# Adding a token's own value on TensorE instead of VectorE in eleven units of an RWKV-then-MoE kernel

## The chip, the cores and the metric

The kernel runs on one core of one Trainium2 chip. The metric is the device time of one execution in microseconds, lower is better; where nothing else is said, a time is in microseconds and counts from the start of the profiled span. The engines are named as in the profile: PE is TensorE, DVE is VectorE, ACT is ScalarE, POOL is GpSimd, SP is SyncE, which issues most of the transfers. PEld is the weight load of PE.

## What is computed

A recurrent attention (RWKV) is followed by a mixture of experts with one expert for each token. The first part, cut to what matters:

```python
for t in range(S):                      # B=4 sequences, H=8 heads, S=768, D=48
    kt, vt, rt = k[:, :, t], v[:, :, t], r[:, :, t]
    cur = einsum('bhd,bhe->bhde', u * kt, vt)
    y[:, :, t] = einsum('bhd,bhde->bhe', rt, state + cur)
    state = w[:, :, None] * state + einsum('bhd,bhe->bhde', kt, vt)
```

The term with `cur` is the token's own: for each head it is the scalar d = sum(r * u * k) times the token's own v. The second part takes x, the heads of y side by side (3072 tokens of 384), and computes `logits = x @ w_gate + modality_bias`, the expert with the greatest logit and its softmax weight, and for each token `weight * (relu(x @ w1[e]) @ w2[e])` of that expert (8 experts, 384 to 1024 to 384).

## The kernel before

The first part works on units: a unit is 128 tokens of one of the 4 sequences, all 8 heads, and there are 24, in the order of the chunks, so that units 0 to 3 are the first chunk. The recurrence is written as products within a chunk, and a state that is handed from chunk to chunk. For each unit PE makes the scores (line 383, into two banks `psc`), DVE masks them (line 389, `at`), and PE sums into one bank, `py`, the state's part (line 413, not in the first chunk) and the chunk's part (line 420). It then makes the new state's part in bank `pst` (line 431; for units 8 to 13 line 426 first adds the faded old state by a product) and, in the same bank, the scalars d of the next unit (line 352, "bonus"). DVE copies d out (line 357), and ACT scales the token's own v by it, head by head, into `dv` (line 369, eight pieces in two halves; from unit 9 to 13 POOL does the second half, line 365).

`token`, the function that changes, makes x: it adds `dv` to `py` (line 439, DVE, 128x384 in f32), and ACT sums the squares of x (line 454). From that sum DVE derives a power of two (lines 287 and 289, `ebx` and `sx`), ACT writes the high half of x as f16 (line 484), DVE the low half (line 488), and SP turns both by a DMA transpose (line 493) for the routing.

A loop of steps runs over the units. In step i the engines get, in this order: the scores of unit i+1; `token` of unit i-1; the copy of d of unit i; the state of unit i-1 out of `pst` (line 469 on ACT in the first chunk, line 467 on DVE later, line 474 on ACT for units 8 to 13); the keys of unit i+2 (line 343); the power of two for unit i-1; the first half of `dv` of unit i; the high half of unit i-1; the masks of unit i+1; the second half of `dv`; the low half of unit i-1 and its transpose; and `values` of unit i, which is lines 413 to 431 and the bonus of unit i+1. Pieces of routing work are put in between at marked places. Each engine runs its own list strictly in this order; the order is written by hand and no scheduler changes it. `py` has two buffers, so the sums of unit i wait until the low half of unit i-2 has been read; `pst` has one.

From step 8 on the mixture of experts starts beside this: the routing tables (lines 637 to 657 on DVE, at the end of step 8), the loads of the first expert's weights (line 852, from SP), their squares (line 855, ACT), their scale (lines 869 and 872) and their split into two f16 halves (lines 885 and 890). Step 13 also runs the first half of an expert's products for the first 128 tokens (line 944) between the scores and `values`.

Ahead of the scores of units 1 to 13 PE runs products that write nothing anybody reads (line 377): 128x128 ones in f16 times 128x512 ones, into the banks that the scores then overwrite. There are 6 for units 1 to 8 and 2 for units 9 to 13.

Of the kernel before, what the change touches and what calls it, by code (L numbers as in the profile page):

```python
# [41 lines left out]
DENSE = 6  # L42
FADED = range(8, 14)
SHARED = range(9, 14)

NE = 9
EARLY = 3
# [12 lines left out]
class _Kernel:  # L60
# [298 lines left out]
    def own(self, i, q):  # L359
        nc, u = self.nc, self.ctx_[i]  # L360
        if q == 0:
            u["dv"] = self.a.tile([P, DM], F32, tag="dv", name=f"dv{i}")
        if q and i in SHARED:
            half = lambda t: t[:, DM // 2 :].rearrange("p (h e) -> p h e", e=D)
# [6 lines left out]
    def scores(self, i):  # L371
        nc, u = self.nc, self.ctx_[i]
        u["ps"] = [self.ps_a.tile([P, 512], F32, tag="big", name=f"psc{i}_{j}") for j in range(2)]
        if 0 < i < BARE:

            for q in range(2 if i - 1 in FADED else DENSE):
                nc.tensor.matmul(u["ps"][q % 2], self.ones16, self.warm, start=True, stop=True)

        for pr in range(NPR):
            for q in range(2):  # L380
                s = slice(64 * q, 64 * q + 64)
                for j, r in enumerate(HALVES):
                    nc.tensor.matmul(u["ps"][j][s, pr * P : (pr + 1) * P], u["kc"][r, pr, s], u["rc"][r, pr, :], start=True, stop=True)  # L383
# [51 lines left out]
    def token(self, i):  # L435
        nc, a, u = self.nc, self.a, self.ctx_[i]
        b, c = self.units[i]
        u["x"] = u["py"][:, :DM]
        nc.vector.tensor_add(u["x"], u["x"], u["dv"])
        n = [hi - lo for lo, hi in GROUPS if lo == i]  # L440
        if n:

            new = lambda n, sh, dt=F32, **k: a.tile(sh, dt, tag=n, name=f"{n}{i}", **k)
            self.grp = dict(
                n=n[0],
                lo=i,
                row=new("row", [P, B, RW], I16, bufs=3),
                xT=new("xT", [P, B, 2 * DC, P], F16),
                ssq=new("ssq", [P, B]),
                sx=new("sx", [P, B]),  # L450
            )
        u["g"], u["at_g"] = self.grp, i - self.grp["lo"]
        u["x16"] = self.grp["row"][:, u["at_g"], : 2 * DM].bitcast(F16)
        nc.scalar.activation(u["x16"][:, :DM], u["x"], AF.Square, accum_out=self.grp["ssq"][:, u["at_g"] : u["at_g"] + 1])
# [981 lines left out]
```

## Time and profile before

| | us |
|---|---|
| median of 3 runs | 363.95 (361.91 to 366.08) |
| the profiled execution | 359.0 |
| its span, first to last instruction | 357.2 |
| PE busy in the span | 334.1 (94%) |
| DVE busy | 227.1 (64%) |
| ACT busy | 172.4 (48%) |
| line 439, 24 of them on DVE, median of one | 0.554 |
| line 377, 58 records on PE, first and last start | 10.3 and 79.1 |

Busy is the share of time in which an engine runs at least one instruction; the units and the routing lie in the first 180 us or so, the experts behind them. A row of the order of time has the start, the length, the engine, the line, what it writes and reads, its shape, how many instructions were merged into the row, and in brackets the idle time of the engine ahead of it with what ended that. A length of several merged rows is from the first one's start to the last one's end.

### The profile page before, as it was taken

How to read it: one execution, taken by the hardware profiler on the slowest of the kernel's cores; microseconds unless marked ns; L12 is line 12 of the kernel's file. 1: busy time of each engine (PE TensorE's matmuls, PEld its weight loads, DVE VectorE, ACT ScalarE, POOL GpSimd, SP SyncE). 2: the span in 40 equal slices, each digit the busy share in tenths (PEclk: the TensorE clock that was granted, in tenths of full speed). 3: DMA queues.
4: the chain of work that ended last, by engine and by line, in shares of the span. 5: the costliest groups of instructions: out<-in, count | busy, mean ns of one | idle time of the engine just before them, and what ended most of it. 6: DMA issues, size and time to landing. Idle time of an engine off the chain costs nothing. (4 is left out here: it accounts for less than half of the span.)

```text
span 357.2 us, 15050 instructions
## 1 busy us (share of the span) xinstructions
PE 334.1 (94%) x5415; PEld 267.0 (75%) x5415; DVE 227.1 (64%) x751; ACT 172.4 (48%) x457; POOL 168.8 (47%) x233
## 2 busy tenths in 40 slices
PE   7989998996999999999999999998999999999792
PEld 3667787776978796988977677776778888777671
DVE  6998999879498958596558733249423233334950
ACT  7469664657466576566432222255222222257620
POOL 8897578747556773444175611136111121111821
PEclk9999999698799999999999999999999999999999
DMA  6999879999947999753345621125721112112120
GB/s 188 279 226 175 180 214 168 330 280 204 237 115 179 231 239 284 173 120 99 92 110 156 247 68 45 44 53 170 245 65 45 44 44 66 44 26 63 22 57 5
DMA packets 60749, 50.29 MB, mean 141 GB/s; under 512 B 46872, under 2 KB 54311, under 8 KB 60448
## 3 DMA queue, kind: packets, MB, share of 16 engines
q1 hardware_dynamic: 57504, 40.21, 50.5%
q0 software_dynamic: 3200, 9.47, 7.3%
q8 instruction: 30, 0.49, 0.6%
q14 instruction: 15, 0.12, 0.1%
HBM read 28.39 MB, written 11.83 MB: 113 GB/s over the span
## 5 line engine op out<-in xcount | busy, mean ns | idle before, releaser
L944 PEld LDWEIGHTS <-whi 128*128 128x128 f16 x1248 | 73.5, 99 | 3.8 <-issue 1.0
L1018 PEld LDWEIGHTS <-hh 128*128 128x128 f16 x416 | 38.9, 98 | 29.9 <-issue 4.4
L944 PE MATMUL phb<-mxT,whi 128*128 128x128 f16 x768 | 50.7, 219 | 0.0
L369 ACT ACTIVATE dv<-kv,d 128x48 f32<-128x48 f32 x172 | 43.0, 324 | 4.2 <-DVE d L357 2.3
L944 PEld LDWEIGHTS <-wlo 128*128 128x128 f16 x624 | 38.4, 99 | 1.5 <-DVE wlo L890 1.5
L336 POOL TENSOR_TENSOR rk<-rc,kc 128x512 f32<-128x512 f32 x20 | 25.9, 1296 | 27.2 <-DVE ebx L287 13.7
L953 DVE SCALAR_TENSOR_TENSOR hl<-phb,hh 128x256 f16<-128x256 f32 (+1 forms) x48 | 24.2, 512 | 22.7 <-ACT hh L948 18.4
L948 ACT ACTIVATE hh<-phb 128x256 f16<-128x256 f32 (+1 forms) x48 | 21.5, 453 | 34.3 <-PE L944 15.0
L324 POOL TENSOR_TENSOR rc<-ud,powr 128x512 f32<-128x512 f32 (+1 forms) x27 | 31.7, 1182 | 9.2 <-DMA ud<-in_pd 7.5
L1028 DVE TENSOR_SCALAR fac<-mt,wf 128x1 f32<-128x1 f32 x17 | 3.6, 212 | 49.1 <-ACT otb L904 45.6
L389 DVE TENSOR_TENSOR at<-psc,mask 128x512 f32<-128x512 f32 x48 | 31.6, 679 | 1.9 <-PE psc L383 1.8
L904 ACT ACTIVATE otb<-po,fac 128x384 f32<-128x384 f32 x16 | 9.2, 577 | 46.0 <-PE phb L944 42.0
L608 POOL DMA_INDIRECT rows<-row,posi x24 | 26.2, 1093 | 11.0 <-issue 3.4
L1023 PEld LDWEIGHTS <-hl 128*128 128x128 f16 x208 | 19.2, 98 | 16.3 <-issue 3.9
L944 PE MATMUL phb<-mxT,wlo 128*128 128x128 f16 x384 | 29.6, 219 | 1.2 <-DVE wlo L890 1.2
L1018 PE MATMUL po<-wlo,hh 128*128 128x384 f16 x136 | 28.0, 326 | 2.7 <-DVE wlo L890 2.6
L913 POOL TENSOR_TENSOR seenb<-otb,putb 128x1 int32<-128x1 int32 x16 | 5.0, 310 | 53.0 <-ACT otb L904 50.2
L383 PE MATMUL psc<-rc,kc 64*64 64x128 f32 (+1 forms) x768 | 28.7, 288 | 0.4 <-DVE kc L343 0.3
L420 PE MATMUL py<-kv,at 128*64 128x48 f32 x768 | 27.1, 224 | 1.5 <-issue 1.5
L383 PEld LDWEIGHTS psc<-rc,kc 64*64 64x64 f32 (+1 forms) x768 | 22.1, 140 | 8.5 <-issue 3.1
L944 PE MATMUL phs<-mxT,whi 128*128 128x128 f16 x432 | 28.4, 224 | 0.0
L890 DVE SCALAR_TENSOR_TENSOR wlo<-raw,ws,whi 128x1024 f16<-128x1024 f32 (+1 forms) x18 | 27.8, 1590 | 0.8 <-ACT whi L885 0.8
(261 smaller groups left out, 672.9 us busy)
## 6 DMA issues: line engine op xcount, KB each, us to landing
ud<-in_pd SPq DMA_DIRECT2D x24, 384.0 KB, 4.3
kv<-in_pt SPq DMA_DIRECT2D x24, 384.0 KB, 5.3
raw<-in_w SPq DMA_DIRECT2D x12, 512.0 KB, 6.4
raw<-in_w SPq DMA_DIRECT2D x2, 1536.0 KB, 6.5
rows<-pad SPq DMA_DIRECT2D x10, 193.0 KB, 2.4
rows<-row,posi POOLq DMA_INDIRECT x24, 5.1
xT<-row SPq DMA_TRANSPOSE x23, 2.8
xn<-rows SPq DMA_TRANSPOSE x17
```

The source lines that it names most:

```text
L324: nc.gpsimd.tensor_mul(u["rc"][:, s], u["rT"][:, s], self.powr[:, s])
L336: (eng or nc.gpsimd).tensor_mul(u["rk"], u["rc"], u["kc"])
L369: nc.scalar.activation(u["dv"][:, sl], u["v"][:, sl], AF.Copy, scale=u["d"][:, h : h + 1])
L383: nc.tensor.matmul(u["ps"][j][s, pr * P : (pr + 1) * P], u["kc"][r, pr, s], u["rc"][r, pr, :], start=True, stop=True)
L389: nc.vector.tensor_mul(u["at"][:, j * NPR : (j + 1) * NPR, :], u["ps"][j].rearrange("p (q t) -> p q t", q=NPR), self.mask.unsqueeze(1).to_ ...
L420: nc.tensor.matmul(py[t, sl], u["at"][:, j * NPR + pr, t], u["v"][:, sl], start=c == h == 0, stop=h == H - 1, skip_group_check=True)
L608: i = nc.gpsimd.indirect_dma_start(out=self.rows, out_offset=bass.IndirectOffsetOnAxis(ap=u["posi"][:, b : b + 1], axis=0), in_=u["row"][: ...
L890: self.nc.vector.scalar_tensor_tensor(self.wlo[:, sl], self.raw[:, sl], sc, self.whi[:, sl], ALU.mult, ALU.subtract)
L944: self.nc.tensor.matmul(ph[:, q * P : (q + 1) * P], w[:, c0 : c0 + P], self.xT[:, xq, t * P : (t + 1) * P], start=i == q == 0, stop=i == l ...
L948: self.nc.scalar.activation(self.hh[:, f0 : f0 + fb, t * P : (t + 1) * P], p3, AF.Relu)
L953: self.nc.vector.scalar_tensor_tensor(self.hl[:, f0 : f0 + fb, r], p3, 0.0, self.hh[:, f0 : f0 + fb, r], ALU.max, ALU.subtract)
L1018: self.nc.tensor.matmul(po[:, :DM], self.hh[:, f, t * P : (t + 1) * P], w[:, c0 : c0 + DM], start=n == q == f == 0, stop=False)
```

## The change

```diff
+ADDED = range(2, 13)
...
-            for q in range(2 if i - 1 in FADED else DENSE):
+            for q in range(1 if i - 1 in FADED else DENSE // 2 if i - 2 in ADDED else DENSE):
                 nc.tensor.matmul(u["ps"][q % 2], self.ones16, self.warm, start=True, stop=True)
...
         u["x"] = u["py"][:, :DM]
-        nc.vector.tensor_add(u["x"], u["x"], u["dv"])
+        if i in ADDED:
+            nc.tensor.matmul(u["x"], self.id32, u["dv"], start=False, stop=True, skip_group_check=True)
+        else:
+            nc.vector.tensor_add(u["x"], u["x"], u["dv"])
```

`DENSE` is 6 and `FADED` is units 8 to 13. In units 2 to 12 the addition on DVE goes, and PE multiplies `dv` by the f32 identity and accumulates onto the bank of `py`. The product stands where `token` is called, so on PE behind the scores of unit i+1 (and, in step 13, behind line 944's products) and ahead of `values`. The products that write nothing become 3 for units 4 to 8 and 1 for units 9 to 13; units 1 to 3 keep their 6. The lines of the changed kernel stand one to four further down.

On PE, in step 4, around the end of the scores of unit 5 (`psc5`) and the start of the sums of unit 4 (`py4`), before:

```order
L383 MATMUL psc5_1_681<-rc5_501,kc5_608 64x128
L413 MATMUL py4_754<-st1_96,rc4_401 64x96 x8
L420 MATMUL py4_754<-kv4_278,at4_627 64x48 x16
L431 MATMUL pst4_779<-kv4_278,kt0_91 64x48
L431 MATMUL pst4_779<-kv4_278,kt0_91 48x48
```

and now, with the product of unit 3:

```order
L384 MATMUL psc5_1_678<-rc5_501,kc5_605 64x128
L441 MATMUL py3_641<-dv3_618,id32_138 128x384
L414 MATMUL py4_748<-st1_96,rc4_401 64x96 x8
L421 MATMUL py4_748<-kv4_278,at4_624 64x48 x16
L432 MATMUL pst4_773<-kv4_278,kt0_91 64x48
L432 MATMUL pst4_773<-kv4_278,kt0_91 48x48
```

The product of the unit before has come in between; it reads `dv3`, which ACT writes in step 3.

On DVE, at the end of step 7 and the start of step 8 (`ebx6` and `sx4` are the power of two, `row4` the low half, `pr0` the routing's sums, `d8` the scalars of unit 8), before:

```order
L287 TENSOR_SCALAR ebx6_1112<-ssq4_827 128x1
L289 TENSOR_SCALAR sx4_828<-ebx6_1112 128x1
L389 TENSOR_TENSOR at8_1126<-psc8_0_1066,mask_143 128x512
L389 TENSOR_TENSOR at8_1126<-psc8_1_1067,mask_143 128x512
L488 SCALAR_TENSOR_TENSOR row4_825<-py6_1016,sx4_828,row4_825 128x384
L439 TENSOR_TENSOR py7_1135<-py7_1135,dv7_1120 128x384
L574 TENSOR_TENSOR pr0_910<-pr0_910,base_160 128x32
L357 COPY d8_1213<-pst7_1160 128x8
```

and now:

```order
L288 TENSOR_SCALAR ebx6_1097<-ssq4_818 128x1
L290 TENSOR_SCALAR sx4_819<-ebx6_1097 128x1
L390 TENSOR_TENSOR at8_1111<-psc8_0_1054,mask_143 128x512
L390 TENSOR_TENSOR at8_1111<-psc8_1_1055,mask_143 128x512
L492 SCALAR_TENSOR_TENSOR row4_816<-py6_1004,sx4_819,row4_816 128x384
L578 TENSOR_TENSOR pr0_901<-pr0_901,base_160 128x32
L358 COPY d8_1197<-pst7_1145 128x8
```

The addition is gone and nothing else has moved: the power of two (line 288 now) still stands ahead of the masks and waits for the sum of squares, which now waits for PE's product.

On PE in step 13, before:

```order
L944 MATMUL phs0_0_1923<-mxT_262,wlo_267 128x128
L869 LDWEIGHTS onesb_145
L869 MATMUL pww2_1973<-wssq_268,onesb_145 128x3
L413 MATMUL py13_2011<-st1_96,rc13_1523 64x96 x8
L420 MATMUL py13_2011<-kv13_1392,at13_1815 64x48 x16
```

and now:

```order
L948 MATMUL phs0_0_1903<-mxT_262,wlo_267 128x128
L441 MATMUL py12_1808<-dv12_1788,id32_138 128x384
L873 LDWEIGHTS onesb_145
L873 MATMUL pww2_1953<-wssq_268,onesb_145 128x3
L414 MATMUL py13_1991<-st1_96,rc13_1505 64x96 x8
L421 MATMUL py13_1991<-kv13_1375,at13_1795 64x48 x16
```

The product of unit 12 stands behind the expert's products and ahead of the sum for the weights' scale.

## The prediction

> **What bounds the kernel now.** I read the page first (its shares are means over stages with different limits), then a table of busy time by step of the loop, and then the order of time around the steps that the change touches. The question is whether TensorE (PE), VectorE (DVE) or ScalarE (ACT) sets the pace in those steps. Step i is one pass of the loop over units. It starts on PE with the empty products ahead of the scores of unit i+1; I cut the trace there, from step 3 (25.66) to step 13 (87.76, which I let run into step 14's scores). The columns are PE, weight loads, DVE, ACT, POOL, then the granted clock.
>
> ```profile
> 25.66:30.05 4.39, 4.39 (x104) 3.31 (x102) 3.20 (x9) 3.85 (x14) 3.67 (x5) 1.00 1.00 198
> 30.05:35.11 5.06, 5.06 (x120) 3.97 (x119) 4.48 (x10) 4.98 (x21) 3.24 (x3) 1.00 0.81 153
> 35.11:41.03 5.92, 5.75 (x145) 4.59 (x143) 5.81 (x14) 3.90 (x15) 2.52 (x4) 1.00 0.67 170
> 41.03:46.07 5.04, 5.04 (x124) 3.95 (x121) 4.95 (x18) 3.92 (x15) 4.77 (x8) 1.00 1.11 242
> 46.07:51.41 5.34, 5.34 (x131) 4.25 (x130) 5.18 (x16) 3.61 (x14) 3.14 (x5) 1.00 0.71 173
> 51.41:56.68 5.27, 5.27 (x129) 4.51 (x126) 5.14 (x19) 3.37 (x13) 4.10 (x5) 1.00 1.13 193
> 56.68:64.74 8.06, 6.31 (x148) 5.39 (x147) 7.78 (x34) 2.43 (x8) 7.39 (x8) 0.90 1.15 233
> ...
> 87.76:100.15 12.39, 12.39 (x219) 11.78 (x218) 6.79 (x16) 6.44 (x14) 8.58 (x9) 0.75 1.11 237
> ```
>
> In steps 3 to 8 PE has no idle time but for 0.17 us in step 5: five of the six rows show busy equal to the length. DVE is nearly as full from step 5 on (5.14 of 5.27 in step 8), but PE never waits for it except in that 0.17. So a VectorE addition taken away there buys nothing by itself, and what PE gains or loses in work goes straight into the time. From step 9 on PE waits, for these things:
>
> ```profile
> 56.40 0.16 DVE L637 SCALAR_TENSOR_TENSOR pr<-pr,idxf 128x8 f32<-128x8 f32 x1
> ...
> 59.66 0.57 DVE L439 TENSOR_TENSOR py<-py,dv 128x384 f32<-128x384 f32 x1
> ...
> 60.26 0.49 ACT L454 ACTIVATE row<-py 128x384 f16<-128x384 f32 x1 [4.00 <-DVE py L439]
> ...
> 60.70 0.15 DVE L357 COPY d<-pst 128x8 f32<-128x8 f32 x1
> ...
> 60.88 0.48 ACT L474 COPY st<-pst 112x384 f32<-112x384 f32 x1
> ...
> 61.41 1.02 PE L426 MATMUL pst<-st,wd 112*112 112x96 f32 x8 [1.36 <-ACT st L474]
> ...
> 78.67 0.16 PE L352 MATMUL pst<-uw,rk 112*64 112x2 f32 x1 [0.80 <-issue]
> ...
> 87.35 0.48 PE L352 MATMUL pst<-uw,rk 112*64 112x2 f32 x6 [3.07 <-issue]
> ```
>
> In step 9 the addition stands on DVE behind the routing work that begins at 56.40; the square waits 4.00 for it, the copy L474 stands behind the square on ACT, and PE's L426 waits 1.36 for that copy. The stalls of 0.80 and 3.07 end by nothing that PE, DVE or ACT does (the releaser is "issue"). Step 13 is gap-free on PE again.
>
> **The change part by part.** Prices first, from these rows of steps 4 and 8.
>
> ```profile
> 30.05 1.47 PE L377 MATMUL psc<-warm 128*128 128x512 f16 x6
> ...
> 31.45 1.10 PE L383 MATMUL psc<-rc,kc 64*64 64x128 f32 x32
> ...
> 51.41 0.59 PE L377 MATMUL psc<-warm 128*128 128x512 f16 x2
> ...
> 51.94 1.10 PE L383 MATMUL psc<-rc,kc 64*64 64x128 f32 x32
> ...
> 52.97 0.88 PE L413 MATMUL py<-st,rc 112*64 112x96 f32 x16
> ...
> 53.68 1.09 PE L420 MATMUL py<-kv,at 128*64 128x48 f32 x32
> ```
>
> An empty product: six hold the scores back by 31.45 - 30.05 = 1.40, two by 0.53, so one costs 0.87/4 = 0.22. Steps 3 to 7 lose three each (-0.66), steps 8 to 12 one each (-0.22).
>
> The f32 product with the identity, which the trace has not: the code issues 8 products at L413 and the row counts 16 records, so an f32 product is streamed twice, and 384 columns become 768. Lower bound: 768 columns at the f16 pace of 0.22 per 512, 0.33. Upper bound: the 8 records of L426 at 61.41 cover the whole array and also make 8 x 96 = 768 columns, in 1.02, with four times as many weight loads. Between them, L413's 16 records use half of the array each; two side by side are again 768 columns, and from its start to the next shape's is 53.68 - 52.97 = 0.71, changes of shape included. I take 0.71, which is also the nearest in kind, and keep 0.33 and 1.02 for the range.
>
> Steps 3 to 8, on PE: six products, +4.26; empty products, 5 x 0.66 + 0.22 = -3.52. Net +0.74.
>
> The addition (0.57 on DVE, 11 times) is hidden now by PE's own work in steps 3 to 8, so taking it away is worth nothing there. But the square now comes after the scores and the product, and everything queued behind it on ACT with it. Step 3:
>
> ```profile
> 26.14 0.49 ACT L454 ACTIVATE row<-py 128x384 f16<-128x384 f32 x1 [1.38 <-DVE py L439]
> ...
> 27.06 1.10 PE L383 MATMUL psc<-rc,kc 64*64 64x128 f32 x32
> ...
> 27.50 0.31 ACT L469 COPY st<-pst 48x192 f32<-48x192 f32 x1
> ...
> 28.09 1.14 PE L420 MATMUL py<-kv,at 128*64 128x48 f32 x32
> ...
> 29.06 0.57 PE L431 MATMUL pst<-kv,kt 128*64 128x48 f32 x15
> ```
>
> The product starts at 28.09 - 0.66 = 27.43, its result is there some 0.88 later (L413's whole length), so the square starts at 28.31 and not at 26.14: 2.17 later. The copy L469 that frees the state's bank is queued behind it and ends at 27.81 + 2.17 = 29.98, where L431 would be ready at 29.06 - 0.66 + 0.71 = 29.11. A new wait of 0.87, which does not exist now; the products of the bonus and the whole next step are queued behind it on PE, and DVE waits for the bonus. The rest of ACT's queue (the token's value for the next product, and the cast that VectorE's low part waits for) is then 2.17 late while PE is only 0.92 late. Step 4 has no room to catch up: ACT is 4.98 of 5.06 busy there. The difference of 1.25 comes back as PE waiting for the token's value at step 4's product or for the low part ahead of step 5's L413, which is where the 0.17 of step 5 lies. Behind the waiting product or L413 stands the rest of the unit on PE, and behind that DVE's next copy of d. I take all 1.25; the ends are 0, if steps 4 and 5 absorb it, and 2.2. In steps 6 to 8 nothing more: ACT is busy 3.4 to 3.9 of over 5 and follows. Sum up to the end of step 8: 0.74 + 0.87 + 1.25 = +2.86.
>
> Step 9: product and empty product, +0.49. The square no longer waits for DVE, so the copy L474 is out of the way early; the other thing that L426 needs is the copy of d at 60.70, which moves with DVE's queue, at most 2.86 later and 0.57 sooner for the addition, to 63.0. PE is there 2.86 + 0.49 after its old arrival at 61.41 - 1.36 = 60.05, at 63.4, so the 1.36 is gone. Net -0.87, sum +1.99.
>
> Steps 10 to 12: +0.49 each, 1.47, priced at nothing, because the stalls of 0.80 and 3.07 stand behind them and end at a time that PE does not set. If that cover goes, +1.47.
>
> Step 13 has no empty products and PE is gap-free through it. Its product stands ahead of the sum of squares that the weights' scale needs, for which DVE waits:
>
> ```profile
> 93.77 0.16 DVE L872 TENSOR_REDUCE wtotw<-pww 128x1 f32<-128x3 f32 x1 [4.87 <-PE pww L869]
> ```
>
> So +0.71, and up to twice that if it runs at half clock. Sum: 1.99 + 0.71 = **+2.7 us**. No queue of SyncE or GpSimd is given or relieved of anything.
>
> **The clock.** It is at half speed twice in these steps. The rows are stretches as long as the clock's own steps, and what follows two of them.
>
> ```profile
> 59.75:63.17 3.42, 2.06 (x49) 1.84 (x45) 3.42 (x14) 2.43 (x8) 3.12 (x3) 1.00 1.21 103
> 63.17:66.58 3.41, 3.02 (x51) 2.08 (x53) 3.16 (x12) 0.46 (x1) 3.11 (x3) 0.50 1.04 393
> 66.58:70.00 3.42, 3.42 (x62) 3.09 (x54) 2.23 (x10) 3.42 (x11) 3.33 (x4) 0.50 1.04 340
> 76.82:80.24 3.42, 2.62 (x70) 2.02 (x73) 3.42 (x9) 1.58 (x3) 0.02 (x1) 1.00 1.03 278
> 83.65:87.06 3.41, 0.63 (x21) 0.54 (x18) 3.24 (x15) 3.36 (x6) 3.26 (x4) 1.00 1.32 215
> 87.06:90.47 3.41, 3.12 (x46) 2.78 (x46) 1.84 (x4) 1.60 (x7) 3.22 (x3) 0.50 1.00 248
> 90.47:93.89 3.42, 3.42 (x36) 3.33 (x35) 0.12 (x1) 0.25 (x2) 1.64 (x3) 0.50 1.27 165
> ```
>
> PE busy 2.06 of 3.42 cost it the clock, 2.62 of 3.42 (with the stall of 0.80 in it) did not. So a stall between about 0.8 and 1.36 decides, and the stall of step 9 is one that this change should remove. The dense products that go are replaced by a longer dense product, so steps 3 to 8 stay busy.
>
> The Trainium skill ("TensorE: Matmul & The Clock Gate", Part 1) says that the clock falls to half only after at least one idle window of about 3.4 us. This trace does not agree: it fell after a window with 2.06 us of work in it, and the measurement decides. By the page's rule no stall here is long enough to cost the clock, before or after, and the sum would stay +2.7 with no rival from the clock; by the rows there is the first rival below.
>
> **The rivals.** Five rows of ACT come first: the state's copies of step 5, the value and the cast of step 8, and two of step 10, where ACT waits for weights.
>
> ```profile
> 35.68 0.79 ACT L401 ACTIVATE st<-st,w 112x192 f32<-112x192 f32 x2
> ...
> 53.08 1.00 ACT L369 ACTIVATE dv<-kv,d 128x48 f32<-128x48 f32 x4
> ...
> 54.78 0.58 ACT L484 ACTIVATE row<-py,sx 128x384 f16<-128x384 f32 x1 [0.70 <-DVE base L584]
> ...
> 66.12 1.06 ACT L855 ACTIVATE junk<-raw 128x1024 f16<-128x1024 f32 x1 [3.39 <-DMA raw<-in_w]
> ...
> 67.64 0.47 ACT L474 COPY st<-pst 112x384 f32<-112x384 f32 x1
> ```
>
> *Faster: both clock cuts stay away.* With the stall of 1.36 gone, the first cut is; 3.02 + 3.42 of work at half clock would take 3.2 less. And if the stall of 3.07 keeps its end while PE arrives 2 later, it shrinks to about 1, and the second cut goes too: 3.12 + 3.42, 3.3 less. Together 2.7 - 6.5 = -3.8. It decides at a stall of about 1 us in both places. Against it: in step 10 ACT waits 3.39 for weights and holds the copy L474 that L426 needs until 67.64, so that PE could use little of the first 3.2, and the second stall may move along with PE.
>
> *Slower by more than 1%: ACT and the product become a loop.* Product, square, four pieces of the token's value, cast, four pieces, next product: 0.88 + 0.48 + 1.0 + 0.58 + 1.0 = 3.9, and two copies of the state, 0.8, in steps 3 to 7, so 4.7 of PE's 5.1. The loop decides when ACT has 0.4 of other work in a step. At 0.5 more in each of steps 5 to 8, and with the cover of steps 10 to 12 gone, it is 2.7 + 2.0 + 1.47 = +6.2. For it speaks step 4, where ACT is full now; against it, that ACT is at most 3.92 of over 5 busy in steps 5 to 8.
>
> *Hidden: the stalls of steps 11 and 12 swallow all that comes before them.* Then only step 13 counts, +0.7.
>
> **How the numbers follow.** The profiled execution took 359.0 (span 357.2, and 1.8 around it), below all three runs (361.91 to 366.08, median 363.95). The forecast against it is 361.7; against the median, 363.95 + 2.7 = 366.65, which I give as 366.6. The rivals: faster 360.1, slower 370.1, hidden 364.7. Chances: forecast 0.40, slower 0.25, hidden 0.17, faster 0.18. One per cent, 3.6 us, is about what a measurement of this kernel can tell from no change. With the bounds of the unknown costs the forecast runs from 364.0 (seven products that nothing covers, each 0.38 cheaper) to 369.8 (each 0.31 dearer, and 2.2 in place of 1.25), and passes 367.6 in a quarter of its cases. So slower by over 1%: 0.25 + 0.10 = 0.35; faster by over 1%: 0.18; within: 0.47. The range, 360.5 to 370.5, leaves out the farther half of the two outer cases; the likeliest one's own is 364.0 to 369.8.
>
> **What would show it.** Steps 3 to 8 still gap-free or nearly so on PE and some 2.9 longer in all; the identity's product 0.7 from start to the next shape; a wait of PE for ACT's L469 in step 3; no wait at L426 in step 9; the stalls without a releaser in steps 11 and 12 shorter by what PE comes later. It is wrong if the product costs under 0.5, if the clock is never cut, or if PE waits for ACT in each of steps 4 to 8.

## The result, and the profile after

| | before | after |
|---|---|---|
| median, range, runs | 363.58 (361.91 to 366.08), 6 | 368.05 (365.38 to 371.86), 6 |
| the profiled execution, its span | 359.0, 357.2 | 367.79, 365.9 |
| PE busy in the span | 334.1 | 341.2 |

The changed kernel takes 1.0143 of the time before (95% interval 1.0098 to 1.0188): 5.2 us more by the ratio, 4.5 by the medians. It is slower, as the forecast with the largest chance had it, but by more than its +2.7. Here and below, a ratio compares only runs within 1.5% of the fastest of their kernel, so it can lie below the ratio of the medians, which count every run.

The table of busy time by step, as in the prediction (PE, weight loads, DVE, ACT, POOL, granted clock), here from step 3 (28.89) to the scores of step 14:

```profile
28.89:34.39 5.50, 4.76 (x103) 3.39 (x102) 2.40 (x8) 2.73 (x11) 3.45 (x3) 1.00 0.47 119
34.39:40.10 5.71, 5.32 (x119) 3.97 (x118) 3.33 (x9) 5.51 (x23) 2.18 (x2) 1.00 0.56 135
40.10:46.25 6.15, 5.94 (x143) 4.59 (x142) 6.04 (x14) 5.07 (x19) 3.21 (x4) 1.00 0.57 143
46.25:51.49 5.24, 5.24 (x123) 3.96 (x120) 4.51 (x16) 3.17 (x13) 4.98 (x7) 1.00 1.12 236
...
57.03:62.92 5.89, 5.89 (x130) 4.77 (x126) 4.79 (x17) 3.00 (x12) 3.45 (x4) 1.00 1.04 236
62.92:69.58 6.66, 6.59 (x149) 5.42 (x148) 6.42 (x28) 2.44 (x8) 6.06 (x6) 1.00 1.09 225
...
75.62:83.08 7.46, 6.42 (x140) 5.19 (x136) 5.07 (x16) 5.31 (x14) 4.13 (x5) 1.00 1.06 316
83.08:91.97 8.89, 6.05 (x129) 4.91 (x126) 8.68 (x33) 6.64 (x15) 6.06 (x6) 1.00 1.22 200
91.97:105.03 13.06, 12.02 (x222) 10.89 (x220) 8.35 (x16) 6.54 (x16) 8.17 (x8) 0.87 0.87 215
```

The first two columns of numbers are to be compared. PE was full in steps 3 to 8 but for 0.17; now it is idle for 0.74 in step 3, 0.39 in step 4 and 0.21 in step 5, and full again in steps 6 to 8. Step 9 has lost its idle time (8.06 - 6.31 = 1.75 before, 0.07 now). Step 11 has 1.04 idle, and so has the last row, step 13. What those waits are, in the order of time (its first row belongs to the clock, below):

```profile
19.63 0.73 PE L421 MATMUL py<-kv,at 128*64 128x48 f32 x18 [1.75 <-issue]
...
30.67 0.91 PE L441 MATMUL py<-dv,id 128*128 128x384 f32 x2
31.51 1.14 PE L421 MATMUL py<-kv,at 128*64 128x48 f32 x32
31.62 0.49 ACT L458 ACTIVATE row<-py 128x384 f16<-128x384 f32 x1 [6.60 <-PE py L441]
...
32.98 0.31 ACT L473 COPY st<-pst 48x192 f32<-48x192 f32 x1
...
33.36 0.48 PEld L432 LDWEIGHTS pst<-kv,kt 128*64 128x64 f32 x15 [0.84 <-issue]
33.39 0.58 PE L432 MATMUL pst<-kv,kt 128*64 128x48 f32 x15 [0.74 <-POOL kt L332]
...
36.64 0.91 PE L441 MATMUL py<-dv,id 128*128 128x384 f32 x2 [0.39 <-ACT dv L370]
...
43.01 0.88 PE L414 MATMUL py<-st,rc 112*64 112x96 f32 x16 [0.21 <-DVE row L492]
...
77.92 0.49 ACT L458 ACTIVATE row<-py 128x384 f16<-128x384 f32 x1 [1.38 <-PE py L441]
...
78.40 0.47 ACT L478 COPY st<-pst 112x384 f32<-112x384 f32 x1
...
78.92 0.16 PE L873 MATMUL pww<-wssq,onesb 128*128 128x3 bf16 x1 [1.04 <-ACT st L478]
...
91.64 0.40 PE L353 MATMUL pst<-uw,rk 112*64 112x2 f32 x8 [2.84 <-issue]
...
98.53 0.17 PE L873 MATMUL pww<-wssq,onesb 128*128 128x3 bf16 x1 [1.04 <-ACT st L478]
```

In step 3 the square (L458) starts behind the product and not, as before, ahead of the scores; the copy L473 is queued behind it and ends at 33.29, and PE's next products into that bank (L432) start right behind it: their weight load at 33.36, after 0.84 without one, and the products at 33.39, after 0.74 of idle time. The profile does not name the copy as what ended this wait; the order of the three times and the last run below do. In step 4 the product itself waits 0.39 for the token's value, in step 5 the sums wait 0.21 for the low half. The rows from 77.92 to 78.92 are a place that the prediction did not see: the sum of the weights' squares (L873) goes into the bank of `pst`, which the copy L478 has to empty first. The copy stands behind the square, the square behind the product, and PE waits 1.04. The same row with the same 1.04 stands in step 13, at 98.53. The row at 91.64, ahead of the bonus of step 12, is a stall whose end nothing in the profile explains.

The product holds PE for 31.51 - 30.67 = 0.84 until the next shape.

The clock, in windows of its own length:

```profile
17.20:20.60 3.40, 1.65 (x53) 1.51 (x51) 2.48 (x6) 2.29 (x9) 3.17 (x3) 1.00 1.06 255
20.60:24.00 3.40, 3.40 (x29) 2.07 (x25) 2.69 (x6) 2.67 (x9) 2.28 (x3) 0.50 1.25 189
24.00:27.40 3.40, 3.40 (x50) 2.45 (x50) 0.74 (x2) 1.02 (x5) 3.25 (x3) 0.50 0.71 198
88.86:92.28 3.42, 0.64 (x20) 0.62 (x23) 3.25 (x15) 3.30 (x6) 3.23 (x3) 1.00 1.28 187
92.28:95.70 3.42, 3.42 (x52) 3.09 (x42) 2.48 (x3) 0.00 (x0) 3.22 (x4) 0.50 1.00 300
```

Step 9 keeps the clock now, and the cut of step 13 lasts one window and not two. But two windows are lost from 20.6 on, ahead of the first changed instruction (28.89): the stall "issue" of 1.75 at 19.63 falls into the window before. The kernel before has one of 1.48 at the same product and kept its clock there in its profile. That cut accounts for nearly all of the 3.23 by which step 3 starts later (step 2 alone is 3.1 longer), and no changed instruction stands ahead of it. The profile before was a lucky one in this place: eleven of the twelve kernels below have a cut between 20 and 28 as well.

The experts' part seems untouched. From the last bonus product of step 13 to the end the profiled execution of after takes 265.6. In the eight kernels that I ran on one chip it is 264.8 to 267.1 whatever was done to the units. On another chip it is 261.1 to 261.6, and in the profile of before 261.7. So some 3.3 of the 4.6 us by which that profile lies below the six runs before may stand in the experts' part: 97.3 (where that product stands in it) + 265 = 362.3 is near a usual run.

The pair of profiles does not show the whole difference either. Steps 3 to 13, from step 2's last bonus product to step 13's, take 71.78 before and 73.45 after, only 1.67 more. The profile before has four windows at half clock in these steps and the one after has one (a mean granted clock of 0.90 and 0.98), so the waits above are partly paid for by the clock in this pair. What the waits cost is read from the runs, below.

### The profile page after: what moved, and what is told of

Read it like the earlier page. It is cut to its first block, busy times and chain, and to the rows that moved or that the text cites. A ratio compares the mean times of both kernels' runs of the same rounds, so it can differ in the third digit from the quotient of the medians.

```text
span 365.9 us, 15039 instructions
## 1 busy us (share of the span) xinstructions
PE 341.2 (93%) x5417; PEld 267.4 (73%) x5417; DVE 226.9 (62%) x740; ACT 172.6 (47%) x457; POOL 168.4 (46%) x233
## 5 line engine op out<-in xcount | busy, mean ns | idle before, releaser
L1022 PEld LDWEIGHTS <-hh 128*128 128x128 f16 x416 | 38.0, 98 | 33.0 <-ACT hh L952 7.6
L458 ACT ACTIVATE row<-py 128x384 f16<-128x384 f32 x24 | 11.7, 489 | 39.7 <-PE py L441 22.0
L1022 PE MATMUL po<-whi,hh 128*128 128x384 f16 x136 | 28.4, 327 | 0.5 <-ACT hh L952 0.5
```

The costliest lines, as they stand in the source:

```text
L1022: self.nc.tensor.matmul(po[:, :DM], self.hh[:, f, t * P : (t + 1) * P], w[:, c0 : c0 + DM], start=n == q == f == 0, stop=False)
```

## The experiments

Theories as put before the runs: **A**, PE's work sets the pace; **B**, the late square does, through ACT's queue; **C**, the clock decides. Each kernel was timed six or twelve times, beside the kernel before on the same chip. In every table the columns are the ratio with its interval, PE's work against the kernel before (empty product 0.22; product 0.84 behind the scores, 0.74 ahead of them, 0.64 if another product follows: see below), and the mean number of windows of 3.41 at half clock in a run, over all runs, worked out as (1 - mean granted clock) x time / (0.5 x 3.41), here and for the kernel before in the same set.

**First set: one part of the change at a time.**

The empty products as before the change, the product as in it:

```diff
-            for q in range(1 if i - 1 in FADED else DENSE // 2 if i - 2 in ADDED else DENSE):
+            for q in range(2 if i - 1 in FADED else DENSE):
```

> The changed kernel with its empty products as before (6 and 2), so that the product with the identity is the only difference from the kernel before. Theory A (PE's own work sets the pace in steps 3 to 8, the product costs 0.84 there and an empty product 0.22): 15 empty products more in steps 3 to 7 and one more in step 8, 3.5 us, longer than the changed kernel, less the 1.5 us in which PE waits for ACT in steps 3 to 5 now: 370 us, about 1.018 times the kernel before. Theory B (the square that comes later, and ACT's queue behind it, set the pace; PE only waits): the empty products fall into waits, and it takes what the changed kernel takes, 368 us. Theory C (the clock is cut more often because there are fewer empty products): faster than the changed kernel, 364 to 366 us.

The halved empty products alone, the addition on DVE for all units:

> The addition stays on VectorE for all units; only the empty products are halved (3 and 1), as in the changed kernel. Theory A: PE gains 3.5 us in steps 3 to 8 at most; DVE, busy 5.14 of 5.27 in step 8, lets through a part of it: 361 to 363 us, 0.992 to 0.998 times the kernel before. Theory B: no difference from the kernel before, 363.6 us. Theory C: slower than before, 366 us or more, with a lower mean clock.

The whole change, but the product issued in `scores`, between the empty products and the scores:

```diff
             for q in range(1 if i - 1 in FADED else DENSE // 2 if i - 2 in ADDED else DENSE):
                 nc.tensor.matmul(u["ps"][q % 2], self.ones16, self.warm, start=True, stop=True)
+        if i - 2 in ADDED:
+            o = self.ctx_[i - 2]
+            nc.tensor.matmul(o["py"][:, :DM], self.id32, o["dv"], start=False, stop=True, skip_group_check=True)
...
-        if i in ADDED:
-            nc.tensor.matmul(u["x"], self.id32, u["dv"], start=False, stop=True, skip_group_check=True)
-        else:
+        if i not in ADDED:
             nc.vector.tensor_add(u["x"], u["x"], u["dv"])
```

> The changed kernel, but the product with the identity is issued between the empty products and the scores of the same step and not behind the scores, so that the square can start 1.0 us sooner (in step 13, 4.9 us sooner, ahead of the expert's products as well). PE does the same work. Theory A: only the waits for ACT in steps 3, 4, 5 (1.5 us) and part of those ahead of the weights' sum in steps 11 and 13 (2.7 us) go, and the product's own 0.84 stays: 365 to 366 us, 1.005 times the kernel before. Theory B: all of the loss goes, 363.6 us. If the product now waits for the token's value, which ACT writes last in the step before, it is no better than the changed kernel, 368 us.

The same place, but the product goes into the bank that the scores overwrite, and DVE adds for all units:

```diff
+        if i - 2 in ADDED:
+            nc.tensor.matmul(u["ps"][0][:, :DM], self.id32, self.ctx_[i - 2]["dv"], start=True, stop=True)
...
-        if i in ADDED:
-            nc.tensor.matmul(u["x"], self.id32, u["dv"], start=False, stop=True, skip_group_check=True)
-        else:
-            nc.vector.tensor_add(u["x"], u["x"], u["dv"])
+        nc.vector.tensor_add(u["x"], u["x"], u["dv"])
```

> As the one that issues the product ahead of the scores, but the product writes into the scores' bank, where the scores overwrite it, and VectorE adds as in the kernel before. PE's work is that of the changed kernel, and the square waits for DVE as before. Theory A: PE's extra work in steps 3 to 8 is 6 x 0.84 - 3.5 = 1.5 us and in step 13 0.84 at full clock, so 365 to 366 us, like the one before it, since the addition on DVE is hidden. Theory B: as the kernel before, 363.6 us. If the relief of DVE was worth something, this one is slower than the one before it, by up to the 0.55 us of each addition that is not hidden.

| kernel | median | ratio | PE's work | windows, before |
|---|---|---|---|---|
| product only, empty products kept | 372.47 | 1.0252 (1.0177 to 1.0327) | +9.2 | 3.2, 3.7 |
| fewer empty products only | 362.97 | 1.0025 (0.9986 to 1.0063) | -4.4 | 4.8, 3.7 |
| product ahead of the scores | 363.80 | 1.0036 (0.9996 to 1.0075) | +3.7 | 2.6, 3.7 |
| product unused, DVE adds | 363.18 | 1.0040 (1.0001 to 1.0079) | +3.7 | 3.1, 3.7 |

The place of the product is worth 1.1 per cent (1.0143 to 1.0036). That does not yet decide between A and B, because the interval of 1.0036 holds A's 1.005 as well as no loss at all. What DVE is spared is worth nothing that can be measured: used or unused, 1.0036 and 1.0040. The two differ in one thing more, though. In the profile of the used product, step 4 has a wait for the token's value, which ACT writes late in the step before:

```profile
34.47 0.91 PE L382 MATMUL py<-dv,id 128*128 128x384 f32 x2 [1.31 <-ACT dv L370]
```

Theory C as first put falls: the kernel that it had below the change is the slowest, and halving the empty products alone did not cost 1%. Theory A is half refuted and half not: 4.4 us less work on PE gain nothing that can be measured (at best 0.14%), while 4.4 us more behind the late product cost 1.1%, more than A had for it. Both have to be explained.

**Second set: where the late product costs, and whether PE's work has a price.** Three kernels leave the product where the change put it, for a part of the units only, with the halved empty products in all:

```diff
-ADDED = range(2, 13)
+THIN = range(2, 13)
+ADDED = range(2, 5)
...
-            for q in range(1 if i - 1 in FADED else DENSE // 2 if i - 2 in ADDED else DENSE):
+            for q in range(1 if i - 1 in FADED else DENSE // 2 if i - 2 in THIN else DENSE):
```

> The changed kernel, with the product (in the place that the change gave it, behind the scores) for units 2 to 4 alone; units 5 to 12 have VectorE's addition again, and all empty products stay halved. Compare with the kernel that has the halved empty products alone (1.0025) and the changed kernel (1.0143); what is split is the 1.2% between them, 4.3 us. Theory B, late square: the waits that the profile showed for these units, 0.9 at L432 in step 3, 0.5 at step 4's product and 0.3 at L414 in step 5, give 1.7 us, so some 364.5, ratio 1.007. Theory A, PE's work sets the pace: three products of 0.84, 2.5 us, 365.3, ratio 1.009. Where neither holds and the loss comes from later steps, 363, ratio 1.002.

With `ADDED = range(5, 12)`:

> The same with the product for units 5 to 11 alone. Theory B: no wait is seen in steps 6 to 9, only the one of some 1.1 us for the scale of the weights' sum in step 11, so 364, ratio 1.005. Theory A: seven products of 0.84 are 5.9 us, of which the stalls of steps 11 and 12 may swallow two, so 366.5 to 368.5, ratio 1.012 to 1.017.

With `ADDED = range(12, 13)`:

> The same with the product for unit 12 alone; in its step the product stands behind the scores and behind the products of the first expert. Theory B: the square is some 4.9 us later than with VectorE's addition, and the sum of squares for the weights' scale waits for ScalarE, 1.1 to 1.3 us, so 364.2, ratio 1.006. Theory A: one product of 0.84, of which none is covered, 363.8, ratio 1.005. If the end of the loop over units is not what the experts wait for, 363, ratio 1.0025.

And the product ahead of the scores with a second one behind it:

```diff
             nc.tensor.matmul(o["py"][:, :DM], self.id32, o["dv"], start=False, stop=True, skip_group_check=True)
+            nc.tensor.matmul(u["ps"][0][:, :DM], self.id32, o["dv"], start=True, stop=True)
```

> The kernel with the product between the empty products and the scores (1.0036), and a second product of the same operands right behind it, whose result goes into the bank of the scores and is overwritten by them. It adds 11 products of 0.84 to PE, 9.2 us, and moves the square of no unit. Theory A, PE's work goes into the time: 363.8 + 9.2, less what the stalls of steps 11 and 12 swallow (some 2.5), 370 to 373, ratio 1.022 to 1.029. Theory B, PE's work is covered and only the place of the square counts: under 366, ratio below 1.010. If A, the earlier result for the product whose result is unused (1.0040) is hard to understand; if B, the third of the empty products that costs 1.1% behind the late product is so only by making the square later still.

| kernel | median | ratio | PE's work | windows, before |
|---|---|---|---|---|
| units 2 to 4 | 363.25 | 1.0058 (1.0015 to 1.0101) | -1.9 | 5.0, 3.4 |
| units 5 to 11 | 361.95 | 1.0017 (0.9976 to 1.0058) | +1.5 | 2.1, 3.4 |
| unit 12 | 363.78 | 1.0056 (1.0014 to 1.0097) | -3.6 | 4.6, 3.4 |
| product twice | 372.28 | 1.0189 (1.0080 to 1.0299) | +10.8 | 3.3, 3.4 |

Units 2 to 4 and unit 12 lie where B had them, but their intervals hold all three expectations: undecided. Units 5 to 11 are clear: seven late products cost nothing that can be seen, against A's 1.012 to 1.017, although the profile has the wait at the weights' sum, 1.04 in step 11 and 1.44 in step 13. It has something to set against that: PE's wait of 2.4 at the state in step 9, which the two other kernels of this kind have, is not in it, and it loses the clock least. Above the 1.0025 of the halved empty products the parts make 0.33 - 0.08 + 0.31 = 0.56%, and the whole change 1.18%. Each of these ratios is known to some 0.4%, and the intervals taken together give 1.1% for this comparison, so it is not shown that the parts cost less than the whole.

The doubled product is nearer to A's: the median, 372.28, is in A's range and 8.5 above that of the single one; the ratio is below A's 1.022, but its interval holds A's range and hardly reaches B's. Its profile also prices the product. The order of time of that kernel, step 6:

```profile
47.39 0.81 PE L378 MATMUL psc<-warm 128*128 128x512 f16 x3
48.04 0.81 PE L382 MATMUL py<-dv,id 128*128 128x384 f32 x2
48.68 0.81 PE L383 MATMUL psc<-dv,id 128*128 128x384 f32 x2
49.42 1.10 PE L389 MATMUL psc<-rc,kc 64*64 64x128 f32 x32
```

From start to start: 0.65 for three empty products, 0.64 for a product followed by another, 0.74 for one followed by the scores. Eleven of 0.64 are 7.0. At about equal clock (0.989 to 0.994) five runs of the single product take 360.4 to 363.9, with 361.9 in the middle, and two of the double one 366.5 and 366.9, some 4.8 more; the other four, 371.5 to 373.6, have a clock of 0.978 to 0.983. By the medians the ratio is 1.0275. So above the change's load PE's work does go into the time, at most of its price and with a dearer clock on top.

What is different below that load is read in the kernel with the halved empty products alone. Its waits on PE in steps 5 and 9, from the order of time:

```profile
39.09 0.88 PE L414 MATMUL py<-st,rc 112*64 112x96 f32 x16 [1.72 <-DVE row L489]
...
61.56 0.49 ACT L455 ACTIVATE row<-py 128x384 f16<-128x384 f32 x1 [4.00 <-DVE py L440]
...
62.19 0.48 ACT L475 COPY st<-pst 112x384 f32<-112x384 f32 x1
...
62.72 1.02 PE L427 MATMUL pst<-st,wd 112*112 112x96 f32 x8 [2.41 <-ACT st L475]
```

and its windows around the second:

```profile
58.55:61.96 3.41, 1.77 (x52) 1.64 (x48) 3.20 (x12) 0.40 (x2) 3.21 (x3) 1.00 1.22 224
61.96:65.38 3.42, 2.66 (x65) 2.55 (x65) 3.42 (x17) 2.04 (x8) 3.01 (x4) 1.00 0.96 280
65.38:68.79 3.41, 3.41 (x51) 2.69 (x49) 2.80 (x12) 2.30 (x7) 3.18 (x4) 0.50 1.01 359
```

What PE no longer does it waits for: 1.72 for DVE's low half in step 5 (0.17 before), 2.41 in step 9 (1.36 before), and after the latter the clock is cut. The wait of step 9 is 2.40 in the kernel with the product for unit 12 alone too, which is the same up to there; the one of step 5 is not in that profile, where the clock was at half for most of step 3. So there is a second chain, DVE's and ACT's, that is hardly shorter than PE's list, and the clock may take part of a gain. That gave theory C a new form: work on PE that fills its waits keeps the clock up and pays for itself. Over the runs of the kernel before, a window more at half clock goes with 0.8 to 1.7 us more time (four sets of runs, slopes of 1.7, 1.3, 1.5 and 0.8).

**Third set: the new theory C against A.** The product for units 5 to 11 alone, ahead of the scores; the halved empty products in all:

> The product for units 5 to 11 alone, ahead of the scores (in steps 6 to 12); VectorE's addition for units 2 to 4 and 12; empty products halved. Over all runs so far, a run's time rises by some 1.4 us for each window of 3.4 us that its mean granted clock has lost; the median loss is 4.5 windows with the halved empty products alone and 2.2 with the product for units 5 to 11 behind the scores. Theory C (the products pay themselves back by keeping the clock): some 2 windows lost again, and the square not late, so at or below the 361.95 of that kernel: 360.5 to 362, ratio 0.995 to 1.000. Theory A (PE's work sets the pace, the clock is chance): seven products of 0.65 over the halved empty products, 365 to 367, ratio 1.009 to 1.015.

The same without any empty product in steps 3 to 12:

```diff
-            for q in range(1 if i - 1 in FADED else DENSE // 2 if i - 2 in THIN else DENSE):
+            for q in range(0 if i - 2 in THIN else 2 if i - 1 in FADED else DENSE):
```

> As the run before it in this call, with no empty product at all in steps 3 to 12 (three fewer in each of steps 3 to 7, one fewer in each of 8 to 12: 20 of 0.22, 4.4 us of PE's work). Theory A: 4.4 us faster than that kernel. Theory C: what PE does not do it waits for, and the clock goes instead: at least one more window lost, within 1.5 us of that kernel, on either side.

The halved empty products alone, but four in each of steps 8 to 12:

```diff
-            for q in range(1 if i - 1 in FADED else DENSE // 2 if i - 2 in ADDED else DENSE):
+            for q in range(4 if i - 1 in FADED else DENSE // 2 if i - 2 in ADDED else DENSE):
```

> VectorE's addition for all units and halved empty products (1.0025, 4.5 windows lost), but in steps 8 to 12 four empty products in place of one, ahead of the stalls: 15 more, 3.3 us of PE's work that computes nothing. Theory C: the stalls of steps 9 to 12 cover them and the clock is lost less often: 3 windows or fewer, 360.5 to 362, ratio 0.995 to 1.000. Theory A: 3.3 us slower than 362.97, ratio 1.010 to 1.012.

| kernel | median | ratio | PE's work | windows, before |
|---|---|---|---|---|
| ahead, units 5 to 11 | 358.59 | 0.9988 (0.9955 to 1.0022) | +0.8 | 3.2, 3.9 |
| the same, no empty products | 360.68 | 0.9989 (0.9942 to 1.0036) | -3.6 | 5.8, 3.9 |
| four late empty products | 359.25 | 0.9999 (0.9958 to 1.0041) | -1.1 | 3.4, 3.9 |

This chip is faster (the kernel before has 358.99), so the ratios count and not the times that were expected. All three ratios are C's, and A's are excluded, also for the second, which it had 1.2% below the first. The windows moved as C has it: 4.4 us less work in the second kernel than in the first, 2.6 windows more at half clock for it, and by the ratios the same time. By the medians it is 2.1 more, which is beyond the 1.5 that C allowed. In the two other kernels C expected fewer lost windows than came: 2 and up to 3, against 3.2 and 3.4. What the runs do not separate is how much of the 4.4 us went into waits and how much into the clock: at 0.8 to 1.7 each, an estimate from the slopes above, 2.6 windows are 2.1 to 4.4 us. The second kernel's profiled execution, at 363.76 one of its longest, shows the trade at one place, PE's wait in step 5 (0.25 in the first kernel's profile) and the windows that follow:

```profile
41.69 1.55 PE L419 MATMUL py<-st,rc 112*64 112x96 f32 x16 [2.48 <-DVE row L495]
```

```profile
37.20:40.60 3.40, 2.01 (x64) 1.75 (x64) 3.40 (x6) 3.15 (x12) 3.09 (x3) 1.00 0.77 226
40.60:44.00 3.40, 2.31 (x36) 2.32 (x38) 3.29 (x10) 1.61 (x7) 0.31 (x1) 0.51 0.38 86
44.00:47.45 3.45, 3.45 (x75) 3.44 (x73) 2.78 (x7) 2.04 (x7) 3.45 (x4) 0.50 0.94 259
47.45:50.87 3.42, 3.42 (x38) 2.01 (x39) 2.03 (x9) 1.94 (x7) 1.79 (x4) 0.50 0.61 148
```

The wait of 2.48 is followed by three windows at half clock; in the first of them PE is still idle for 1.1. None of the three is measurably faster than the kernel before.

**Last run: the late square by itself.** Putting the product ahead of the scores had moved two things, the square and the work on PE. So the product stays where the change put it, but writes into the bank of the next unit's `py`, whose own first product overwrites it, and DVE adds as before:

```diff
-        py = u["py"] = self.ps_y.tile([P, 512], F32, tag="y", name=f"py{i}")
+        py = u["py"] if i - 1 in ADDED else self.ps_y.tile([P, 512], F32, tag="y", name=f"py{i}")
+        u["py"] = py
...
         if i in ADDED:
-            nc.tensor.matmul(u["x"], self.id32, u["dv"], start=False, stop=True, skip_group_check=True)
-        else:
-            nc.vector.tensor_add(u["x"], u["x"], u["dv"])
+            py = self.ctx_[i + 1]["py"] = self.ps_y.tile([P, 512], F32, tag="y", name=f"py{i + 1}")
+            nc.tensor.matmul(py[:, :DM], self.id32, u["dv"], start=True, stop=True, skip_group_check=True)
+        nc.vector.tensor_add(u["x"], u["x"], u["dv"])
```

> The changed kernel's products on TensorE, at the same place of its order behind the scores and with the same halved empty products, but written into the bank of the next unit's y, where that unit's own first product overwrites them; the token's own value is added by VectorE as before the change, so the square does not wait for the scores and the product. It has the changed kernel's work on TensorE in its order, and the square, the copies and the norms as early as before. Theory B, the late square is what costs: as the product ahead of the scores, ratio 1.001 to 1.007. Theory A, work on PE behind the scores costs more than ahead of them, whoever waits for it: as the changed kernel, 1.010 to 1.019.

It took 363.90, ratio 1.0059 (1.0023 to 1.0095), with 2.6 windows against 3.8 before. That is B's, and A's range lies above the interval. Its order of time in steps 3 and 11:

```profile
29.16 0.49 ACT L459 ACTIVATE row<-py 128x384 f16<-128x384 f32 x1 [3.91 <-DVE py L444]
...
30.51 0.31 ACT L474 COPY st<-pst 48x192 f32<-48x192 f32 x1
...
31.02 0.91 PE L443 MATMUL py<-dv,id 128*128 128x384 f32 x2
...
31.86 1.14 PE L422 MATMUL py<-kv,at 128*64 128x48 f32 x32
...
32.83 0.57 PE L433 MATMUL pst<-kv,kt 128*64 128x48 f32 x15
...
74.41 0.48 ACT L479 COPY st<-pst 112x384 f32<-112x384 f32 x1 [0.19 <-DVE d L358]
...
75.44 0.91 PE L443 MATMUL py<-dv,id 128*128 128x384 f32 x2
...
76.19 0.17 PE L874 MATMUL pww<-wssq,onesb 128*128 128x3 bf16 x1
```

The product is there, 0.84 and 0.75 up to the next start, and none of the five waits is: the copies are done before PE gets to the products that need their bank (30.82 for 32.83, 74.89 for 76.19). In the changed kernel the five add up to 0.74 + 0.39 + 0.21 + 1.04 + 1.04 = 3.4, and the two ratios differ by 0.84% of 362, 3.0 (1.0 to 5.1, the two intervals taken together). The profiles agree: steps 3 to 13 are 73.45 with the change and 71.40 here, 2.05 apart although this kernel has two windows at half clock in them and the changed one has one. What is left, 0.59% or some 2.1 us, is the price of the products and of the halved empty products without the late square. The lengths of some steps, from one unit's last bonus product to the next one's, show the rest:

```
step         before   product ahead   product behind,   product behind,
                      of scores       unused            the change
   3          4.39        4.39            4.59              5.50
   4          5.05        6.63            5.25              5.71
   5          5.30        5.05            5.25              5.53
   6          5.66        5.66            5.85              5.85
   7          5.05        5.05            5.25              5.25
```

Step 4 is longest with the product ahead of the scores, because of the wait of 1.31: that place has a wait of its own. Steps 6 and 7 have no waits in any of the four. There three empty products less and a product ahead of the scores leave the step as it was, and behind the scores make it 0.20 longer.

## Why the prediction was right, and where it was short

*PE full in steps 3 to 8, what it gains or loses "goes straight into the time".* Right upwards, wrong downwards. Above the old load the doubled product costs most of its price. Below it PE waits for DVE and ACT instead, and 4.4 us less bought nothing that could be measured. Full on PE, with work that computes nothing among it, meant that PE's list was about as long as the other chain, not that it was the only bound.

*"A VectorE addition taken away there buys nothing by itself."* Right as far as the runs can tell: 1.0036 without and 1.0040 with the addition on DVE, each known to 0.4%.

*The product at 0.71.* It is 0.84 where the change puts it and 0.64 to 0.74 ahead of the scores. The prediction took the columns as streamed twice; at the pace of an empty product, 0.22 for 512 columns, 0.64 is the time of some 1490 columns, nearer to four times 384, so the lower bound of 0.33 was far too low. With 0.84 the net of steps 3 to 8 is 6 x 0.84 - 3.52 = +1.52, against the +0.74 that stood there.

*The waits of steps 3 to 5.* The new wait of 0.87 for L469's copy came as 0.74 on PE (0.84 on its weight load), at the place named. The 1.25 behind it, at step 4's product or step 5's L413, came at both places, as 0.39 and 0.21 (0.17 of it was there before): over-sized threefold. With the dearer product, steps 3 to 8 are 3.01 longer by the starts of their empty products, and the forecast was 2.86: a sum that came out right by luck, since the product was priced too low and the waits behind step 3 too high.

*Step 9, -0.87.* The sign and the wait were right, L426's 1.36 is gone. The step became 1.40 shorter, since a wait of 0.39 for a transfer went too and its clock is whole.

*Steps 10 to 12 covered, step 13 +0.71.* This is the step that failed. The stalls were priced as ending at a time that PE does not set. The one ahead of the bonus in step 12 hardly shrank (3.07 before, 2.84 after), so it covered 0.23 at most and moves along with PE; the one of 0.80 in step 11 is not in the profile after. And in front of it, in step 11, and again in step 13, stands a wait that does not exist before, 1.04 each, at the sum of squares for the weights' scale. The prediction followed the square's lateness down ACT's queue only in steps 3 to 5 and took it as settled from step 6 on, because ACT was not full; but a late item needs no full queue to make someone wait, only a bank that is wanted soon after. The two waits, 2.08, are about what +2.7 lacked against the measured 4.5 to 5.2. That they are the very amount is not shown: the clock hides a part in the pair of profiles, and the kernel with the product for units 5 to 11 has both waits (1.04 and 1.44) at no cost that can be seen.

*The rivals.* "Both clock cuts stay away": the first did, the second was halved, and another two windows were lost in a place that the change does not touch. The six runs after have a mean clock of 0.985, 3.2 windows, against 3.4 to 3.9 in the runs of the kernel before in the four sets, so the clock was not cut more often with the change. The page of the Trainium skill that the prediction weighed ("TensorE: Matmul & The Clock Gate", Part 1: the clock falls after an idle window) is contradicted here again, by the cut after 2.66 of 3.42 in the kernel with the halved empty products. The prediction's own rule, that a stall between about 0.8 and 1.36 decides, does not hold either. In the profile with the product for units 5 to 11 the clock stayed whole through a stall of 2.10 that fell into two windows (busy 2.44 and 2.04), and the kernel with the halved empty products kept it after 1.77. What did not stand in the prediction as a term is that the lost windows go with the load itself. "ACT and the product become a loop": no wait of PE in steps 6 to 8, so not. "Hidden by the stalls": not.

Open: whether the late product for units 2 to 4, for 5 to 11 and for 12 really costs less apart than together, what in a window decides about the clock, and how the single lost window comes to cost 0.8 us in one set of runs and 1.7 in another.

## What to carry to other kernels

Follow a late result down the whole queue of the engine that takes it, through every step, and ask of each item which buffer it empties and who wants that next; of the 5.2 us here some 3.0 were five waits of 0.2 to 1.0, and the added products themselves were the smaller part. When an engine is full of work that computes nothing, take a part of that work away on the chip before calling the engine the bound: here 4.4 us of it were worth nothing that could be measured. And if work has to move to another engine, put it in the order of that engine where its operands are there and its result is wanted, not where the old instruction stood in the code: the same change costs 0.4% with the product ahead of the scores and 1.4% behind them.

## What the runs showed of the chip that was not expected

- The same f32 product of 128x128 by 384 holds PE for 0.64, 0.74 or 0.84 until the next start, depending on what stands ahead of it and behind it.
- A run's mean granted clock goes with the load: 4.6 to 5.8 windows at half speed where PE's work was cut by 1.9 to 4.4 us, 2.1 to 3.4 where it was from -1.1 to +10.8, and 3.4 to 3.9 in the kernel before. The busy share of one window does not decide: cuts came after windows with PE busy 0.64, 1.65, 2.01 and 2.66 of some 3.4, and windows with 1.77, 2.04 and 2.44 kept the clock.
- PE stalls without a releaser (0.4 to 3.1) stand at the same few places in most of the kernels, and they can bring a cut that no changed instruction causes. In the profiles before and after, each ends 2 to 3 us after a 16 KB transfer of an instruction queue (q8) has started, near 17, 76 and 85 before, near 17 and 89 after. Most of these transfers, one every 5 to 10 us, have no stall behind them, and that they are the cause is not shown.
- The part behind the units takes 261 to 262 on one chip and 265 to 267 on two others, with the same work in it.
